# A second column piece of 36 instead of 26 in the score matmuls of 90-row blocks

## The chip, the cores and the metric

The kernel runs on one core of a Trainium2 chip. The metric is the device time of one execution in microseconds (us). The kernel before takes 801.79 us, the median of three runs (801.49 to 802.13).

## The reference

Talking-heads attention is followed by a gated feed-forward layer. Batch is 4, heads 12, sequence 448, head dimension 64; the inputs are 32-bit floats.

```python
scores = scale * np.matmul(q, k.transpose(0, 1, 3, 2))
scores = np.einsum('bhij,hg->bgij', scores, w_pre)
attn = np.exp(scores - np.max(scores, axis=-1, keepdims=True))
attn = attn / (np.sum(attn, axis=-1, keepdims=True) + 1e-09)
attn = np.einsum('bhij,hg->bgij', attn, w_post)
x = np.matmul(attn, v)                      # then as 1792 x 768
gate = 1.0 / (1.0 + np.exp(-(x @ w_gate)))
out = gate * (x @ w_val) @ w_out
```

## The kernel before, in words

The attention comes first (up to about 345 us), the feed-forward layer after it. The query rows of each batch are cut into four blocks of 120, 120, 120 and 88 rows. Rows are worked on in sets of ten (`R`), so the last block of a batch holds nine sets and carries 90 rows, two of them twice. There are 16 blocks, and four of them (one for each batch) have 90 rows.

`scores(bi, c, sc)` (line 151) computes q times k for one block and one pair of heads. The two heads of a pair lie in partitions 0 to 63 and 64 to 127 of the tiles `q` and `k` (`e` is 0 or 1). The block's rows are the columns of the stationary operand. They are cut into two pieces, 0 to 64 and 64 to `n`, and the results of both pieces go to one PSUM bank, to partitions 0 to 63 and from 64 on. So one call issues four matmuls, piece by piece and in each piece head by head: (first piece, e=0), (first, e=1), (second, e=0), (second, e=1). A matmul of 32-bit floats appears as two weight loads and two matmul records in the trace, so one call, a "score group" below, has eight of each. A block has six groups. For blocks of 120 rows the second piece has 56 columns, for blocks of 90 rows it has 26.

`keep` (line 159) copies the first `n` rows of each score bank to SBUF (`st`), on ScalarE for e=0 and on VectorE for e=1. `regroup` (line 195) lets DMAs on SyncE's queue bring `st` into the tile `T`, where heads and rows of two sets lie in the partitions; `premix` (line 205) mixes the heads by matmuls into the banks `pm`; `rowmax` takes the row maxima (VectorE, `nm`), `expo` the exponentials (ScalarE, `e`), `norm` and `scale` the division (GpSimd, `ss` and `ph`), `p_lo` the low part (VectorE, `pl`), `postmix` (line 243) mixes the heads again (TensorE, `mx`), `mix` (line 257) copies that out of PSUM (ScalarE), and `av` (line 272) multiplies by v, with its result copied out on ScalarE (`xt`).

All this runs in slots, one for each unit of two sets; the order inside a slot is written out by hand in the loop at line 396. In slot s TensorE gets premix(s+2), one score group of the next block but one, postmix(s), and one `av`, in this order. ScalarE gets the first exponential of s+2, the copy of scores, the second exponential, in some slots a sum of absolute values over v (`v_sum`, tile `v_abs`), then mix(s), and in some slots `xt`. `mx` is a single buffer, so postmix(s+1) starts when mix(s) is done. SyncE issues the loads of q, k, v and weights and the `regroup` DMAs in the order of the slots.

`q_load` (line 140) loads a block's q into a tile of 720 columns, of which a 90-row block uses 540 (pair c in columns 90c to 90c+89). There are two such tiles.

Of the kernel before, what the change touches and what calls it, by code (L numbers as in the profile page):

```python
# [32 lines left out]
def _sets(n):  # L33

    return [min(r0, n - R) for r0 in range(0, n, R)]
# [6 lines left out]
def _attention(ctx, tc, ins, B, H, S, D, xs, raws, make_moe):  # L42

    nc = tc.nc
    qp, kp, vb = (ins[n] for n in ("qp", "kp", "vb"))
    NQ = H // QUAD
    NP = H // 2
# [69 lines left out]
    for b in range(B):  # L117
        for i0, n in _blocks(S):
            rows = _sets(n)
# [13 lines left out]
    k_t, q_t = {}, {}  # L133
# [6 lines left out]
    def q_load(bi, eng=None):  # L140

        b, i0, _, _, sets = blocks[bi]
        n = R * sets
        t = qst.tile([128, NP * QB], F32, tag="q", name="q")
        (eng or nc.sync).dma_start(out=t[:, :NP * n], in_=qp[b, :, NP * i0:NP * (i0 + n)])
        q_t[bi] = t[:, :NP * n].rearrange("p (c s) -> p c s", s=n)


    st_t = {}
# [1 line left out]
    def scores(bi, c, sc):  # L151
        b, n = blocks[bi][0], R * blocks[bi][4]
        q, k = q_t[bi], k_t[b, c]
        for s0, s1 in ((0, 64), (64, n)):
            for e in range(2):
                rows = slice(64 * e, 64 * e + 64)
                nc.tensor.matmul(sc[e][s0:s1, :S], lhsT=q[rows, c, s0:s1], rhs=k[rows, :], start=True, stop=True)  # L157

    def keep(bi, c, e, sc):
        n = R * blocks[bi][4]  # L160
# [148 lines left out]
    for b in range(B):  # L309
# [3 lines left out]
        s = f + 5  # L313
        for i in range(H // 2):
            s = max(s + 1, f + 6 + 2 * (2 * i // QUAD))
# [10 lines left out]
    for bi in range(1, NBK):  # L326
        s0, s1 = first[bi - 1] - LEAD, first[bi] - LEAD
        for c in range(NP):
            at(spread(c, NP, s0, s1), scores, bi, c)
        if bi > 1:  # L330
            at(s0 - 4, q_load, bi)
    for bi in range(NBK):
        s0 = first[bi + 1]
        s1 = first[bi + 2] if bi + 2 < len(first) else s0
# [29 lines left out]

    k_load(0, 0, nc.sync)
    q_load(0, nc.sync)
    for c in range(1, NP):
        k_load(0, c, nc.sync)
    mix_in = load_mix()
    q_load(1, nc.scalar)  # L370
    warm(10)
    todo = []

    def ahead(c):
        if c % 3 == 0:
            mx = two_banks(ps_mx, "mx")
            sc = [mx[:, e] for e in range(2)]
        else:
            sc = pm[:2] if c % 3 == 1 else qk_banks()
        scores(0, c, sc)  # L380
        todo.append(sc)
# [14 lines left out]
    for s in range(min(min(plan), -LEAD), max(plan) + 1):  # L396
# [14 lines left out]
        def job(bi, c):  # L411
            sc = qk_banks()
            scores(bi, c, sc)
            return lambda e: keep(bi, c, e, sc)
# [56 lines left out]
class _Moe:  # L471
# [14 lines left out]
    NP = 7  # L486
# [797 lines left out]
```

## Time and profile before

| | |
|---|---|
| median of 3 runs | 801.79 us |
| the profiled execution | 802.14 us |
| its span from the first to the last instruction | 800.4 us |
| TensorE busy | 778.9 us |
| VectorE busy | 638.3 us |
| ScalarE busy | 566.1 us |
| GpSimd busy | 292.6 us |
| granted TensorE clock, mean | 0.996 |

The profile names engines PE (TensorE matmuls), PEld (its weight loads), DVE (VectorE), ACT (ScalarE), POOL (GpSimd) and SP (SyncE, which issues DMAs). A name such as L157 is a line of the kernel. A busy TensorE isn't one at its peak: matmuls overlap one another in the array, and a stretch in which they follow one by one counts as busy all the same. So of a group of matmuls the distance from its first start to the next group's start is to be read, and not the duration of one record.

### The profile page before, as it was taken

What the parts mean: (1) busy time and instruction counts of PE and PEld (TensorE: products, weight loads), DVE (VectorE), ACT (ScalarE), POOL (GpSimd) and SP (SyncE); (2) the same over time, 40 slices, a digit from 0 to 9 for tenths busy, and PEclk for the clock granted to TensorE, in tenths of its full rate; (3) what the DMA queues carried; (4) which work ended last, traced back from release to release, by engine and by line L of the source; (5) the groups of instructions that cost most, each with busy time, mean ns of one, the idle gap of its engine ahead of it and who ended that gap; (6) DMA issues with size and microseconds to landing.
All of it is one profiled execution on the core that took longest, in us unless ns stands there. A gap on an engine that the chain in (4) does not pass through costs nothing.

```text
span 800.4 us, 23490 instructions
## 1 busy us (share of the span) xinstructions
PE 778.9 (97%) x9626; PEld 418.8 (52%) x9626; DVE 638.3 (80%) x1068; ACT 566.1 (71%) x1106; POOL 292.6 (37%) x462
## 2 busy tenths in 40 slices
PE   8899999999999999978999999999999999999998
PEld 2445655555555655555555555555555555555554
DVE  4977999799978897889998989679886899997111
ACT  3887888888989898878876868568766784553000
POOL 1546666666765654420222232233322212010000
PEclk9999999999999999989999999999999999999999
DMA  5786577757886474665725364665557788995001
GB/s 196 218 233 226 172 237 235 250 173 225 247 254 214 165 238 163 206 170 183 237 76 194 131 218 171 250 214 187 203 153 279 271 306 310 366 381 213 35 35 69
DMA packets 80715, 166.15 MB, mean 208 GB/s; under 512 B 20448, under 2 KB 57664, under 8 KB 80608
## 3 DMA queue, kind: packets, MB, share of 16 engines
q1 hardware_dynamic: 72304, 132.88, 50.6%
q0 software_dynamic: 7728, 31.27, 10.2%
q8 instruction: 75, 1.23, 0.6%
q10 hardware_dynamic: 576, 0.51, 0.2%
q14 instruction: 32, 0.26, 0.1%
HBM read 87.77 MB, written 38.15 MB: 157 GB/s over the span
## 4 chain that ended last, share of the span: by engine, by line
PE 84%; ACT 7%; DVE 5%; DMA 1%; issue 1%; POOL 1%; SPq 0%; ACTq 0%; DVEq 0%; POOLq 0%
PE bank L1138 34%; PE bank L1149 18%; PE qk L157 9%; PE av L280 9%; PE pm L211 7%; PE mx L253 6%; ACT e L223 3%; DVE nm L216 2%; ACT mix L261 1%; DVE pl L241 1%; ACT st L163 1%; ACT m L1117 1%; DVE m L1122 1%; DMA k<-in_kp_dram 1%; DVE st L163 0%
## 5 line engine op out<-in xcount | busy, mean ns | idle before, releaser
L1138 PEld LDWEIGHTS <-m 128*128 128x128 f16 x1512 | 147.8, 98 | 142.1 <-DVE m L1122 3.5
L1138 PE MATMUL bank<-m,m 128*128 128x448 f16 x1116 | 214.4, 352 | 2.7 <-DVE m L1122 2.6
L223 ACT ACTIVATE e<-pm,nm 128x448 f32<-128x448 f32 x180 | 115.2, 641 | 46.8 <-DVE nm L216 44.0
L235 POOL TENSOR_SCALAR ph<-e,ss 128x448 f16<-128x448 f32 x180 | 113.3, 641 | 50.3 <-DVE ss L229 32.8
L216 DVE TENSOR_REDUCE nm<-pm 128x1 f32<-128x448 f32 x180 | 103.5, 616 | 23.9 <-PE pm L211 22.6
L241 DVE SCALAR_TENSOR_TENSOR pl<-e,ss,ph 128x448 f16<-128x448 f32 x180 | 120.8, 710 | 1.2 <-POOL ph L235 1.2
L157 PE MATMUL qk<-k,q 64*64 64x448 f32 (+1 forms) x736 | 112.6, 541 | 2.1 <-ACT st L163 2.1
L1149 PEld LDWEIGHTS <-m 128*128 128x128 f16 x756 | 74.0, 98 | 69.0
L253 PEld LDWEIGHTS <-ph 64*128 64x128 f16 x2880 | 64.6, 93 | 73.6 <-POOL ph L235 33.3
L261 ACT ACTIVATE mix<-mx 128x960 f32<-128x960 f32 (+1 forms) x92 | 102.9, 1119 | 0.2 <-PE mx L253 0.2
L211 PE MATMUL pm<-T,w 64*64 64x448 f32 (+1 forms) x720 | 95.2, 560 | 0.7 <-ACT e L223 0.7
L280 PE MATMUL av<-mix,v 128*64 128x120 f32 (+1 forms) x1504 | 93.3, 269 | 1.4 <-ACT xt L290 1.4
L1149 PE MATMUL bank<-m,m 128*128 128x448 f16 x468 | 92.9, 352 | 0.0
L1075 POOL CAST raws<-raws 128x768 f16<-128x768 bf16 x36 | 37.6, 1045 | 119.3 <-ACT raws L1069 119.3
L253 PE MATMUL mx<-w2hi,ph 64*128 64x60 f16 x1440 | 70.9, 188 | 8.8 <-ACT mix L261 8.5
L1138 PE MATMUL bank<-m 128*128 128x448 f16 x396 | 78.7, 355 | 0.0
L280 PEld LDWEIGHTS av<-mix,v 128*64 128x64 f32 x1504 | 74.1, 138 | 6.1 <-ACT xt L290 1.7
L228 POOL TENSOR_SCALAR ss<-ss 128x2 f32<-128x2 f32 (+1 forms) x92 | 37.4, 407 | 101.2 <-ACT e L223 99.6
L253 PE MATMUL mx<-w2hi,pl 64*128 64x60 f16 x1440 | 70.1, 187 | 0.8 <-DVE st L163 0.8
L253 PE MATMUL mx<-w2lo,ph 64*128 64x60 f16 x1440 | 70.2, 187 | 0.0
L163 DVE COPY st<-qk 120x448 f32<-120x448 f32 (+1 forms) x92 | 56.8, 618 | 13.5 <-PE qk L157 13.1
L1165 DVE TENSOR_TENSOR m<-bank,m 128x448 f32<-128x448 f32 x72 | 44.6, 621 | 22.9 <-PE bank L1138 14.7
(125 smaller groups left out, 1085.0 us busy)
## 6 DMA issues: line engine op xcount, KB each, us to landing
T<-st SPq DMA_DIRECT2D x176, 210.0 KB
m<-w SPq DMA_DIRECT2D x60, 384.0 KB
raws<-in_w_dram SPq DMA_DIRECT2D x28, 767.6 KB
hs<-m POOLq DMA_DIRECT2D x48, 224.0 KB, 3.5
m<-hs SPq DMA_DIRECT2D x15, 672.0 KB
w<-m POOLq DMA_DIRECT2D x21, 384.0 KB, 4.3
w<-raws POOLq DMA_DIRECT2D x20, 384.0 KB, 4.6
v<-in_vb_dram SPq DMA_DIRECT2D x12, 512.0 KB
```

Of the source, the lines that this page charges most:

```text
L157: nc.tensor.matmul(sc[e][s0:s1, :S], lhsT=q[rows, c, s0:s1], rhs=k[rows, :], start=True, stop=True)
L163: (nc.vector.tensor_copy if e else nc.scalar.copy)(st_t[bi][:n, 2 * c + e], sc[e][:n, :S])
L211: nc.tensor.matmul(pm[bank][64 * x:64 * x + 64, :S], lhsT=w1[rows], rhs=T[rows, x], start=True, stop=True)
L216: nc.vector.tensor_reduce(nm[:, i:i + 1], pm[bank][:, :S], axis=AX.X, op=ALU.max, negate=True)
L223: nc.scalar.activation(out=e_t[u][:, i], in_=pm[units[u][2][i]][:, :S], func=AF.Exp, bias=nm_t[u][:, i:i + 1], scale=1.0, accum_out=ss_t[u ...
L235: nc.gpsimd.tensor_scalar(ph[:, i], e_t[u][:, i], ss_t[u][:, i:i + 1], 1.0, op0=ALU.mult, op1=ALU.mult)
L241: nc.vector.scalar_tensor_tensor(pl[:, i], e_t[u][:, i], ss_t[u][:, i:i + 1], p_t[u][0][:, i], op0=ALU.mult, op1=ALU.subtract)
L253: nc.tensor.matmul(mx[:, x, i, jb * HK:(jb + 1) * HK], lhsT=p[rows, i, JB[jb]:JB[jb] + 128], rhs=w[rows], start=(k == 0), stop=(k == 2))
L261: nc.scalar.activation(out=out.rearrange("p g (y r) -> p y g r", r=HALF), in_=mx_t.pop(u), func=AF.Copy, scale=1.0 / (P_UP * W_UP))
L280: nc.tensor.matmul(av_t[bi][64 * i:64 * i + 64, c % 4, :n], lhsT=vt[b, u][:, h + i, jb, :], rhs=mixes[bi % 2][:, jb, 2 * c + i, :n], start ...
L1138: self.nc.tensor.matmul(self.f32(bank), lhsT=w[a][:, k], rhs=x[b][:, k], start=self.START[i] and k == r == 0, stop=k == self.KH - 1 and r ...
L1149: self.nc.tensor.matmul(self.f32(bank), lhsT=w[a][:, k], rhs=b[bb], start=self.START[i] and j == k == r == 0, stop=j == OUT_TILES - 1 and ...
```

## The change

For blocks of fewer than 100 rows the second column piece of the scores ends at column 100 instead of 90: it is 36 columns wide instead of 26. The ten further columns belong to the next pair of heads in the q tile; for the last pair they lie behind the loaded data, and a new GpSimd memset sets these ten columns to zero. The further results go to partitions 90 to 99 of the score banks, and `keep` doesn't copy them. Blocks of 120 rows issue what they did before.

```diff
@@ q_load
-        q_t[bi] = t[:, :NP * n].rearrange("p (c s) -> p c s", s=n)
+        if n < 100:
+            nc.gpsimd.memset(t[:, NP * n:NP * n + 100 - n], 0.0)
+        q_t[bi] = [t[:, c * n:] for c in range(NP)]
@@ scores
-        for s0, s1 in ((0, 64), (64, n)):
+        for s0, s1 in ((0, 64), (64, max(n, 100))):
             for e in range(2):
                 rows = slice(64 * e, 64 * e + 64)
-                nc.tensor.matmul(sc[e][s0:s1, :S], lhsT=q[rows, c, s0:s1], rhs=k[rows, :], start=True, stop=True)
+                nc.tensor.matmul(sc[e][s0:s1, :S], lhsT=q[c][rows, s0:s1], rhs=k[rows, :], start=True, stop=True)
```

## Rows read from the trace of the kernel before

**Rows 1.** The page: busy time by engine, and the chain of waits by engine.
```profile
PE 778.9 (97%) x9626; PEld 418.8 (52%) x9626; DVE 638.3 (80%) x1068; ACT 566.1 (71%) x1106; POOL 292.6 (37%) x462
PE 84%; ACT 7%; DVE 5%; DMA 1%; issue 1%; POOL 1%; SPq 0%; ACTq 0%; DVEq 0%; POOLq 0%
```

**Rows 2.** Groups by shape, line 157: count | busy us, mean ns | idle before.
```profile
L157 PE MATMUL qk<-k,q 64*56 64x448 f32 x272 | 65.3, 540 | 0.0
...
L157 PE MATMUL qk<-k,q 64*26 64x448 f32 x96 | 22.5, 545 | 0.0
...
L157 PEld LDWEIGHTS qk<-k,q 64*56 64x56 f32 x272 | 17.8, 127 | 0.0
...
L157 PEld LDWEIGHTS qk<-k,q 64*26 64x26 f32 x96 | 3.1, 99 | 16.9 <-issue 16.9
```

**Rows 3.** Timeline of PE, two slots with 120-row scores: start us, us, what.
```profile
252.56 0.93 PE L157 MATMUL qk<-k,q 64*64 64x448 f32 x8
253.42 0.20 PE L253 MATMUL mx<-w2hi,ph 64*128 64x60 f16 x2
...
255.96 0.93 PE L157 MATMUL qk<-k,q 64*64 64x448 f32 x8
```

**Rows 4.** Timeline of PE, then PEld, a slot with 90-row scores.
```profile
139.20 1.79 PE L157 MATMUL qk<-k,q 64*64 64x448 f32 x8
...
143.46 0.92 PE L157 MATMUL qk<-k,q 64*64 64x448 f32 x4
...
140.05 0.13 PEld L157 LDWEIGHTS qk<-k,q 64*26 64x26 f32 x4 [0.70 <-issue]
```

**Rows 5.** Four 90-row windows, one 120-row: busy PE, PEld, DVE, ACT, POOL; clock, DMA.
```profile
44.87:71.35 26.48, 25.72 (x485) 12.97 (x483) 18.81 (x37) 22.34 (x50) 14.03 (x21) 1.00 0.77 221
130.69:156.23 25.54, 25.54 (x485) 12.92 (x483) 19.78 (x40) 22.30 (x53) 15.45 (x24) 1.00 0.83 259
215.31:240.87 25.56, 25.56 (x484) 12.96 (x482) 19.67 (x40) 21.47 (x53) 15.75 (x24) 1.00 0.83 250
299.43:324.98 25.55, 25.55 (x484) 12.77 (x478) 19.68 (x45) 22.26 (x49) 11.54 (x18) 1.00 0.45 156
246.00:263.00 17.00, 17.00 (x412) 10.70 (x408) 15.18 (x31) 15.49 (x36) 10.69 (x19) 1.00 0.62 197
```

**Rows 6.** Timeline of ACT, one 90-row slot and the next one's start.
```profile
146.94 1.11 ACT L261 ACTIVATE mix<-mx 128x960 f32<-128x960 f32 x1
148.72 0.63 ACT L223 ACTIVATE e<-pm,nm 128x448 f32<-128x448 f32 x1 [0.66 <-DVE nm L216]
...
149.53 0.53 ACT L163 COPY st<-qk 90x448 f32<-90x448 f32 x1
...
151.19 1.12 ACT L261 ACTIVATE mix<-mx 128x960 f32<-128x960 f32 x1
152.17 0.44 ACT L290 ACTIVATE xt<-av,sw 128x240 f32<-128x240 f32 x1
```

**Rows 7.** Waits in 215.31:240.87: us in total, times, longest us.
```profile
PEld pm L211 <- DMA T<-st: 0.6, 1, 0.6
```

**Rows 8.** Groups: the memsets on POOL.
```profile
L193 POOL MEMSET T<- 4x896 f32 x4 | 3.2, 835 | 0.3 <-POOLq L1270 0.3
...
L1270 POOL MEMSET const-float32-1.0<- 128x1 f32 x1 | 0.1, 99 | 0.0
```

**Rows 9.** Timeline, POOL and SP around the third 90-row load of q.
```profile
202.29 0.62 SPq L145 DMA_DIRECT2D q<-in_qp_dram  x1
202.60 1.26 POOL L235 TENSOR_SCALAR ph<-e,ss 128x448 f16<-128x448 f32 x2 [0.37 <-DVE ss L229]
```

**Rows 10.** The page, DMA issues: KB each, median us to landing.
```profile
w<-raws POOLq DMA_DIRECT2D x20, 384.0 KB, 4.6
```

**Rows 11.** Windows: early slots with an idling PE, and the attention's end.
```profile
25.49:41.00 15.51, 13.80 (x327) 8.04 (x325) 15.08 (x32) 14.31 (x31) 7.98 (x15) 1.00 0.73 210
350.00:360.00 10.00, 6.94 (x144) 5.70 (x136) 8.36 (x10) 8.69 (x13) 2.43 (x4) 0.72 0.18 54
```

## The prediction

> **What bounds the kernel now.** I read the page first, then the groups of line 157 with shapes kept apart, then the timeline of TensorE around one score group of each kind, then the busy time by stretch, and last what ScalarE and the DMA queues do in the stretches that change. The page says that TensorE is busy for 97% of the span and that 84% of the chain of waits lies on it [rows 1]. That alone doesn't say that its time is well spent. The groups by shape look harmless too: a score matmul with 26 columns takes 545 ns, one with 56 columns 540 [rows 2]. What differs is when they start. In a 120-row slot the whole score group lasts 0.93 us, and postmix starts 0.86 us after the group's start [rows 3]: all four matmuls of a pass run side by side. In a 90-row slot the group lasts 1.79 us [rows 4], and its narrow weight loads stand idle for 0.70 us until the first piece has run through. So the 26-wide piece doesn't run beside the 64-wide one; it runs after it. The 96 narrow weight loads together show 16.9 us of such idle time [rows 2].
>
> The same 0.86 us stands in the slot's period: 4.26 us from score group to score group with 90 rows (139.20 to 143.46), 3.40 us with 120 rows (252.56 to 255.96) [rows 3, 4]. TensorE shows no idle time in three of the four 90-row stretches, and 0.76 us in the first [rows 5]. These stretches are thus bound by TensorE today, and by a TensorE that does two things one after the other which it does at once elsewhere.
>
> **What the change removes.** 96 records of the 26-wide matmul, four for each group, make 24 groups. If the 36-wide piece runs beside the 64-wide one as the 56-wide does, each group loses 1.79 - 0.93 = 0.86 us, in all 24 x 0.86 = 20.6 us of TensorE time. The trace has no piece of 36 columns. The bounds are nothing (it behaves as 26) and 0.86 us (it behaves as 56). I take the latter, though 26 is the nearer number: what the two rows differ in is whether the piece runs beside a 64-wide one, and more columns can only take it toward the kind that does. The duration of a record doesn't grow (540 against 545 ns) and a weight load, between 99 ns (26 columns) and 127 (56) [rows 2], lies under running matmuls in the 120-row slots, so it costs nothing there. If that cover were missing, 96 loads by 0.03 us would be 3 us.
>
> The Trainium skill, TensorEngine Tiling (Array Packing), sections "Available Configurations" and "Key Properties", lists column tiles of 128, 64 and 32 and says that a change of the tiling mode, not merely of the tile, drains the engine. By it 26 columns make a 32-wide tile and 36 a 64-wide one, which is the mode of the first piece, and the sum would be the full 0.86 us a group. No run here shows a width between 26 and 56.
>
> **What is late next.** ScalarE. In a 90-row slot with `v_abs` it goes from mix to mix in 4.25 us (146.94 to 151.19) and waits 0.66 us of that for the row maxima [rows 6], which wait for TensorE. That leaves 3.59 us; about 0.1 of it is the copy `st` standing for the end of the score group, since it starts 0.81 us after an exponential that lasts 0.63. So ScalarE needs some 3.5 us where TensorE would need 3.40, and where an `xt` of 0.44 us follows mix [rows 6], up to 3.9. `mx` has one buffer, so a late mix holds the next postmix and with it all of TensorE. Over a whole stretch: ScalarE is busy for 22.34, 22.30, 21.47 and 22.26 us [rows 5], with seven mixes where six belong to six slots; less one of 1.12 us [rows 6] that is 20.3 to 21.2 us. TensorE would need 25.55 - 6 x 0.86 = 20.4 us. The two take turns in being late, and neither fills the other's gaps entirely, so I take 21.5 us, 0.3 above ScalarE's own work. A stretch then gains 25.55 - 21.5 = 4.05 us, the first one as much (its 0.76 us of waiting stays), and four gain 16.2 us. VectorE's 19.8 us [rows 5] fit in 21.5.
>
> The same page of the Trainium skill, section "PSUM Bottleneck", says that tiling speeds up TensorE but not the copies out of PSUM, which may become the bottleneck. The rows on ScalarE agree, and by them 4.4 of the 20.6 us are lost.
>
> **The DMA queues** come after that. They are busy for 0.77, 0.83, 0.83 and 0.45 of these stretches [rows 5]. The same packets in 21.5 us would take 0.83 x 25.55 / 21.5 = 0.99 in the second and the third. The third already has one wait of premix for its DMA, 0.6 us [rows 7], so there is no reserve there. The cost lies between nothing (loads slide into the emptier slots that follow, 0.62 in a 120-row stretch [rows 5]) and the whole gain of those two, 8.1 us. I take 1.8 us, an estimate: 1.2 in the third, twice its wait of today, and 0.6 in the second. That leaves 16.2 - 1.8 = 14.4 us.
>
> **What it adds.** Four memsets of 128 x 10 on GpSimd. The nearest rows are 99 ns for 128 x 1 and 835 ns for 4 x 896 [rows 8]; I take 0.1 us. GpSimd is busy for 63% of a 120-row stretch [rows 5], so this is hidden; without that cover it would be at most 4 x 0.84 = 3.3 us, and it can't gain, being work added. The memset also stands in GpSimd's queue behind `scale` and ahead of later `norm` and `scale`. Its tile was last read by scores some three slots earlier, so it waits for nothing there. If it waited for the q load before it, though, GpSimd would stand: in the third case SyncE issues that load at 202.29 and `ph` ends at 203.86 [rows 9]; with the 4.6 us that a DMA of 384 KB takes to land [rows 10] that is some 3 us, and `ph`, `pl` and postmix behind it. The columns are disjoint, so I take nothing and keep 4 x 3 = 12 us as the other end. The last pair's second piece waits for the memset, three slots and more after it; nothing. Copies still take 90 rows, so no engine but TensorE has more to write.
>
> **The sum.** The profiled run of before took 802.14 us, a span of 800.4 and 1.7 around it; 802.14 - 14.4 = 787.7. It lies 0.35 above the median, so against the median the forecast is 787.4 us. What follows the attention is moved, not changed: it is bound by TensorE or by its own waits.
>
> **The rivals.**
> 1. TensorE alone bounds: ScalarE's and the DMAs' excess is absorbed by neighbouring slots. 801.8 - 20.6 = 781.2 us. For it: TensorE, VectorE and ScalarE all run nearly full in 120-row slots already. Against it: the single buffer of `mx`.
> 2. DMAs bound the second and third stretch, which keep 1 us of gain each, and the first keeps 3: 801.8 - (3 + 1 + 1 + 4) = 792.8 us. For it: 0.99 of the queues and the wait [rows 5, 7]. The memset that waits for its load would end in the same place or a little lower.
> 3. 36 columns don't run beside 64 either: 801.8 us. For it only that no row shows this width.
> 4. Slower: TensorE, no longer bound, idles for ScalarE, and the chip grants it the half clock. It does so once, at the attention's end, where the mean is 0.72 with TensorE busy for 6.94 of 10 us [rows 11]. A slot of 3.40 us at 1.2 GHz takes 3.40 us more, so 14.4 / 3.4 = 4.2 of the 24 slots decide; half of them would end at 787.4 + 12 x 3.4 = 828 us. Against it: between 25 and 41 us TensorE was busy for 13.80 of 15.51 us, idler than it would be here, at a clock of 1.00 [rows 11].
>
> **How the numbers follow.** Forecast (ScalarE and some DMA) 0.64, its own range 784.5 to 790.5; rival 1 0.11; rival 2 0.14; rival 3 0.08; rival 4 0.03. The range from 781.5 to 793.5 takes in the forecast and most of rivals 1 and 2 and leaves out 3 and 4 and some of the tails, about 0.18. A measurement of this kernel can tell about 0.2% (1.6 us) from no change. Faster: 0.64 + 0.11 + 0.14 = 0.89; same 0.08; slower 0.03.
>
> **What would show it.** The score group of 90 rows lasts 0.93 us and the idle time of its narrow weight loads is gone: else the first step is wrong. Stretches of six slots take 21.5 us, with new waits of postmix for mix: 20.4 would mean rival 1. Waits of premix for T in the second and third stretch above 2 us in all mean rival 2. A wait of the memset for the q load, or a clock under 1.00 in these stretches, would be a cost that I put at nothing. The gain must stand whole at the attention's end; if the end of the program moves by less, the step "moved, not changed" fails.

## The result

The changed kernel takes 789.19 us, the median of five runs (787.11 to 791.72), where the kernel before took 801.49 (800.71 to 802.13) on the same chip: a ratio of 0.9847 with a 95% interval of 0.9825 to 0.9870, a gain of 12.3 us. The forecast was 787.4 us with a range of 781.5 to 793.5 and 0.89 for faster. The profiled execution of after is the slowest of the five (791.72 us, span 789.9), so a second sample of the same kernel stands among the experiments (e5_again).

The page of after, busy time by engine and the chain of waits, answers to [rows 1]:

```profile
PE 763.4 (97%) x9626; PEld 419.5 (53%) x9626; DVE 637.1 (81%) x1068; ACT 562.3 (71%) x1106; POOL 287.6 (36%) x466
...
PE 75%; ACT 10%; DVE 6%; DMA 5%; POOL 2%; issue 2%; SPq 0%; ACTq 0%; DVEq 0%; POOLq 0%
```

TensorE's busy time fell by 15.5 us, and its share of the chain from 84% to 75%. What rose are DMA (1 to 5%) and ScalarE (7 to 10%). The lines of the code stand two further down than before (L157 is L159, L163 is L165, L261 is L263).

The score matmuls by shape, against [rows 2] (count | busy us, mean ns | idle before):

```profile
L159 PE MATMUL qk<-k,q 64*56 64x448 f32 x272 | 65.3, 540 | 0.0
L159 PE MATMUL qk<-k,q 64*36 64x448 f32 x96 | 22.2, 538 | 0.0
...
L159 PEld LDWEIGHTS qk<-k,q 64*36 64x36 f32 x96 | 5.8, 113 | 1.5 <-issue 0.9
```

The record of the narrow piece lasts as long as it did (538 against 545 ns). What is gone is the idle time ahead of its weight loads, 1.5 us instead of 16.9. The timeline of TensorE in a slot with scores of 90 rows shows the same, against [rows 4] (start us, us, what):

```profile
135.62 0.93 PE L159 MATMUL qk<-k,q 64*64 64x448 f32 x8
136.48 0.20 PE L255 MATMUL mx<-w2hi,ph 64*128 64x60 f16 x2
...
139.02 0.78 PE L159 MATMUL qk<-k,q 64*64 64x448 f32 x4
```

The group lasts 0.93 us, postmix starts 0.86 us after it, and this slot's period is 3.40 us: all three are the numbers of a 120-row slot [rows 3].

The four stretches with scores of 90 rows, cut at the starts of the same score groups as in [rows 5] (window, length; busy PE, PEld, DVE, ACT, POOL; clock, DMA share, GB/s). Behind the last group of the fourth no score group follows; that stretch ends where one would start, 0.81 us after the start of the next premix, which gives the 324.98 of [rows 5] in the kernel before:

```profile
44.94:67.88 22.94, 21.59 (x483) 12.87 (x479) 18.43 (x36) 20.67 (x50) 11.55 (x20) 1.00 0.82 231
128.41:150.34 21.93, 21.15 (x483) 13.25 (x479) 19.39 (x39) 20.41 (x51) 13.89 (x23) 1.00 0.88 275
209.76:234.78 25.02, 22.70 (x485) 13.27 (x481) 19.70 (x40) 20.83 (x53) 16.37 (x24) 0.93 0.79 247
293.35:314.54 21.19, 20.66 (x484) 12.28 (x476) 18.80 (x43) 20.91 (x49) 9.44 (x18) 1.00 0.52 175
```

They were 26.48, 25.54, 25.56 and 25.55 us long. So they gained 3.54, 3.61, 0.54 and 4.36 us, 12.05 in all. Between them the other slots lost: from the end of the first to the start of the second it is now 60.53 us (67.88 to 128.41) where it was 59.34, then 59.42 where it was 59.08, then 58.57 where it was 58.56, together 1.54 us. The start lost 0.07, and what follows the last stretch 0.02. The sum is 10.42 us, the difference of the two spans (800.36 and 789.94). The second and the fourth stretch are near the 21.5 us of the forecast; the third kept nearly nothing of the gain. Three places tell why.

First, ScalarE, which keeps even the undisturbed fourth stretch above the 20.4 us that TensorE would need. A slot of the second stretch, from mix to mix (start us, us, what):

```profile
138.89 1.13 ACT L263 ACTIVATE mix<-mx 128x960 f32<-128x960 f32 x1
139.87 0.65 ACT L292 ACTIVATE xt<-av,sw 128x480 f32<-128x480 f32 x1
...
142.04 0.66 ACT L178 ACTIVATE v_abs<-v 128x512 bf16<-128x512 f32 x1
...
142.65 1.15 ACT L263 ACTIVATE mix<-mx 128x960 f32<-128x960 f32 x1
```

Nothing stands in brackets, also on the lines left out: ScalarE works without a pause for 3.76 us from one mix to the next, where it waited 0.66 us in a slot of before [rows 6]. It is the late engine of such a slot. TensorE's waits for mix between 44 and 322 us, before and after (us in total, times, longest), are the sign that the prediction named for this:

```profile
PE mx L253 <- ACT mix L261: 0.9, 4, 0.3
...
PE mx L255 <- ACT mix L263: 3.3, 13, 0.3
```

Second, the first stretch. ScalarE's timeline, TensorE's, and SyncE's issues:

```profile
65.59 0.46 ACT L292 ACTIVATE xt<-av,sw 128x240 f32<-128x240 f32 x1 [1.67 <-DMA xs<-xt]
```

```profile
66.10 1.04 PE L282 MATMUL av<-mix,v 128*64 128x120 f32 x16 [1.08 <-ACT xt L292]
```

```profile
59.25 0.39 SPq L271 DMA_DIRECT2D xs<-xt  x1
```

The buffer of `xt` is free once the store of its last content has landed. That store was issued at 59.25 and still held the buffer at 65.5; ScalarE stood for 1.67 us, and TensorE, which needs the bank that `xt` empties, for 1.08. The kernel before had a wait of this kind too, once between 44 and 322 us, and after has two (us in total, times, longest):

```profile
ACT xt L290 <- DMA xs<-xt: 0.7, 1, 0.7
...
ACT xt L292 <- DMA xs<-xt: 2.7, 2, 1.7
```

Third, the third stretch. TensorE's timeline:

```profile
222.41 0.43 PE L282 MATMUL av<-mix,v 128*64 128x120 f32 x4
224.79 1.47 PE L282 MATMUL av<-mix,v 128*64 128x120 f32 x12 [1.95 <-issue]
226.19 1.77 PE L213 MATMUL pm<-T,w 64*64 64x448 f32 x8
```

The window around the place (columns as for the stretches):

```profile
224.00:228.10 4.10, 3.31 (x24) 1.86 (x28) 0.20 (x2) 1.12 (x3) 3.13 (x5) 0.58 0.74 265
```

In the middle of an `av` TensorE stops for 1.95 us, and no engine and no data DMA is named for it ("issue": no releaser shows). At its end the granted clock falls to half: a mean of 0.58 over 4.10 us is some 3.4 us at 1.2 GHz, in which premix takes 1.77 us instead of 0.98. The wait and half of 3.4 us, an estimate of what the half clock cost, come to 3.65 us, all that this stretch has over 21.4.

### The profile page after: what moved, and what is told of

Same layout as the page of the kernel before. It is cut to its first block, busy times and chain, and to the rows that moved or that the text cites. A ratio compares the mean times of both kernels' runs of the same rounds, so it can differ in the third digit from the quotient of the medians.

```text
span 789.9 us, 23497 instructions
## 1 busy us (share of the span) xinstructions
PE 763.4 (97%) x9626; PEld 419.5 (53%) x9626; DVE 637.1 (81%) x1068; ACT 562.3 (71%) x1106; POOL 287.6 (36%) x466
## 3 DMA queue, kind: packets, MB, share of 16 engines
q8 instruction: 75, 1.23, 0.7%
## 4 chain that ended last, share of the span: by engine, by line
PE 75%; ACT 10%; DVE 6%; DMA 5%; POOL 2%; issue 2%; SPq 0%; ACTq 0%; DVEq 0%; POOLq 0%
PE bank L1140 34%; PE bank L1151 18%; PE av L282 7%; PE pm L213 6%; PE qk L159 5%; PE mx L255 5%; ACT e L225 4%; ACT mix L263 2%; DVE nm L218 2%; DMA T<-st 2%; DMA xs<-xt 2%; DVE pl L243 1%; ACT st L165 1%; ACT v_abs L178 1%; DVE m L1124 1%
## 5 line engine op out<-in xcount | busy, mean ns | idle before, releaser
L263 ACT ACTIVATE mix<-mx 128x960 f32<-128x960 f32 (+1 forms) x92 | 103.0, 1119 | 0.2 <-PE mx L255 0.2
L213 PE MATMUL pm<-T,w 64*64 64x448 f32 (+1 forms) x720 | 97.5, 565 | 0.7 <-ACT e L225 0.7
L159 PE MATMUL qk<-k,q 64*64 64x448 f32 x736 | 95.1, 540 | 2.0 <-ACT st L165 1.8
L230 POOL TENSOR_SCALAR ss<-ss 128x2 f32<-128x2 f32 (+1 forms) x92 | 30.8, 335 | 95.7 <-ACT e L225 94.0
L1167 DVE TENSOR_TENSOR m<-bank,m 128x448 f32<-128x448 f32 x72 | 44.6, 621 | 22.7 <-PE bank L1140 14.4
L255 PEld LDWEIGHTS <-pl 64*128 64x128 f16 x1440 | 61.4, 93 | 0.0
```

What stands on the lines that cost most here:

```text
L159: nc.tensor.matmul(sc[e][s0:s1, :S], lhsT=q[c][rows, s0:s1], rhs=k[rows, :], start=True, stop=True)
L213: nc.tensor.matmul(pm[bank][64 * x:64 * x + 64, :S], lhsT=w1[rows], rhs=T[rows, x], start=True, stop=True)
L255: nc.tensor.matmul(mx[:, x, i, jb * HK:(jb + 1) * HK], lhsT=p[rows, i, JB[jb]:JB[jb] + 128], rhs=w[rows], start=(k == 0), stop=(k == 2))
L263: nc.scalar.activation(out=out.rearrange("p g (y r) -> p y g r", r=HALF), in_=mx_t.pop(u), func=AF.Copy, scale=1.0 / (P_UP * W_UP))
L1167: self.nc.vector.tensor_tensor(self.f32(out), self.f32(bank), self.f32(snap), op=ALU.add)
```

## The experiments

Their stretches, in us, from the same windows as above, and the sum of the three pieces between them (each window is cut at the starts of the same score groups, the end of the fourth as said above):

| kernel | 1st | 2nd | 3rd | 4th | between | time, median |
|---|---|---|---|---|---|---|
| before | 26.48 | 25.54 | 25.56 | 25.55 | 176.98 | 801.49 |
| after | 22.94 | 21.93 | 25.02 | 21.19 | 178.52 | 789.19 |
| e5_again (after once more) | 21.89 | 22.73 | 22.90 | 21.20 | 179.01 | 789.36 |
| e2_w33 (33 wide) | 21.43 | 21.48 | 24.03 | 21.26 | 177.90 | 788.12 |
| e3_vlate (sums of v later) | 21.76 | 23.15 | 24.97 | 20.43 | 181.01 | 794.90 |
| e4_kearly (k loaded earlier) | 23.74 | 21.20 | 25.51 | 21.22 | 178.22 | 790.38 |
| e6_no_vsum | 22.12 | 20.70 | 23.10 | 21.37 | 177.14 | 787.25 |
| e7_no_reload | 22.91 | 21.38 | 22.03 | 21.20 | 178.94 | 788.10 |
| e8_no_both | 22.32 | 20.42 | 21.91 | 20.42 | 178.83 | 787.21 |
| e9_xfer_after | 21.20 | 25.92 | 24.07 | 21.65 | 178.39 | 791.10 |
| e10_xfer_before | 25.54 | 25.54 | 25.54 | 25.55 | 177.00 | 801.52 |
| e11_half_sums | 21.07 | 21.36 | 24.34 | 21.59 | 180.77 | 791.11 |

### Where does a piece begin to run beside its neighbour?

```diff
-        if n < 100:
-            nc.gpsimd.memset(t[:, NP * n:NP * n + 100 - n], 0.0)
+        if n < 96:
+            nc.gpsimd.memset(t[:, NP * n:NP * n + 96 - n], 0.0)
...
-        for s0, s1 in ((0, 64), (64, max(n, 100))):
+        for s0, s1 in ((0, 64), (64, max(n, 96))):
```

That is e1_w32, a second piece of 32 columns. e2_w33 has 97 in the place of 96, a piece of 33.

> The second piece is 32 columns wide. Theory one (a piece of up to 32 columns can't run beside a 64-wide one, whatever its exact width): the score group of 90 rows still lasts 1.79 us and the time is that of before, 801.5 us. Rival (more columns help by degrees, or any width above 26 will do): the group is shorter, some 0.9 to 1.4 us, and the time lies between 789 and 796 us.

> The second piece is 33 columns wide, one more than in the run before it. Theory one (32 is the edge): the score group lasts 0.93 us and the time is that of the changed kernel, 787 to 791 us. Rival (the edge lies elsewhere, between 33 and 36): 1.79 us and 801.5 us.

Measured: 801.16 us with 32 columns (ratio 0.9997, 0.9987 to 1.0006) and 788.12 with 33 (0.9845, 0.9820 to 0.9871). The score matmuls by shape, with 32 columns:

```profile
L159 PE MATMUL qk<-k,q 64*32 64x448 f32 x96 | 22.6, 548 | 0.0
L159 PEld LDWEIGHTS qk<-k,q 64*32 64x32 f32 x96 | 3.4, 104 | 16.9 <-issue 16.9
```

and with 33:

```profile
L159 PE MATMUL qk<-k,q 64*33 64x448 f32 x96 | 22.1, 536 | 0.0
L159 PEld LDWEIGHTS qk<-k,q 64*33 64x33 f32 x96 | 5.6, 108 | 1.0 <-issue 0.7
```

One column turns the 16.9 us of idle weight loads into 1.0, and 13.0 us of the kernel's time go with it. The edge lies between 32 and 33, and at this edge the time is a step: 32 columns cost what 26 did, 33 gain what 36 do. The Trainium skill, TensorEngine Tiling (Array Packing), section "Available Configurations", lists column tiles of 32, 64 and 128. The step agrees with it: up to 32 columns make one kind of tile, from 33 on the kind that the first piece has. What exactly makes the narrow piece wait isn't shown; the runs show that it waits, and at which width it stops.

### Is it the sums over v, or the loads of k?

e3_vlate moves the six sums of |v| of each batch behind the slots with 90-row scores:

```diff
-        s = f + 5
+        s = f + 12
...
-            s = max(s + 1, f + 6 + 2 * (2 * i // QUAD))
+            s = s + 1
```

e4_kearly moves the loads of k out of the slots ahead of and in the stretches:

```diff
-            at(spread(c, NP, first[PB * (b - 1)] + 6, first[PB * b - 1] - LEAD - 2), k_load, b, c)
+            at(spread(c, NP, max(first[PB * (b - 1)] - 10, 1), first[PB * (b - 1)] + 6), k_load, b, c)
```

> The changed kernel, with the six sums of absolute values over v of each batch moved behind the slots with 90-row scores, into 120-row slots. Theory one (ScalarE is what is late in the 90-row slots): slots that take 3.4 and 3.65 us in turn go to 3.40, each of the four stretches gains 0.5 to 1 us, and the time falls by 2 to 4 us against the changed kernel. Theory two (the DMA queues are what is late): under 1 us.

> The changed kernel, with the k loads of the second to fourth batch issued some 11 to 16 slots earlier, out of the 90-row slots. Theory one (ScalarE alone costs the missing part): under 1 us. Theory two (full DMA queues in the first three 90-row stretches hold premix, the copy out of av and the instructions of TensorE): the waits for T and for xs vanish, the third stretch loses its stall, and the time falls by 3 to 5 us against the changed kernel, to 784 to 786.

Measured: 794.90 us for the later sums (ratio 0.9930, 0.9907 to 0.9954), worse than the changed kernel; 790.38 for the earlier loads (0.9868, 0.9839 to 0.9898), no difference that can be told. The window of e3_vlate's fourth stretch:

```profile
296.27:316.70 20.43, 20.43 (x484) 11.99 (x476) 18.75 (x42) 17.55 (x39) 9.53 (x18) 1.00 0.56 187
```

The window of e4_kearly's third stretch, and from its timeline TensorE's longest wait there:

```profile
209.97:235.48 25.51, 22.78 (x485) 13.27 (x481) 19.79 (x40) 21.12 (x53) 15.56 (x24) 0.93 0.66 207
```

```profile
225.47 0.83 PE L282 MATMUL av<-mix,v 128*64 128x120 f32 x10 [2.16 <-issue]
```

Neither theory had forecast a loss for the later sums. With ScalarE rid of the sums (17.55 us busy instead of 20.91), the fourth stretch goes at TensorE's pace. But the sums are only elsewhere: the slots between the stretches grow by 2.5 us against the changed kernel (181.01 against 178.52), so in these slots ScalarE had no room for them either. That is less than the 5.7 us between the medians; what makes up the rest isn't shown. In e4_kearly the third stretch keeps its long wait "issue", in the same `av` as in the changed kernel and two weight loads later, with the DMA share down from 0.79 to 0.66; and the first stretch grows to 23.74 us, with waits of premix for T of 0.67 and 0.42 us. So the average load of the queues in a stretch doesn't decide on that wait.

### The changed kernel again, without the sums, without the reloads, without both

e5_again is the changed kernel. e6_no_vsum leaves out the sums:

```diff
+    nc.gpsimd.memset(vm, 64.0)
...
-            at(s, v_sum, b, i)
```

e7_no_reload leaves out 20 loads of raw weights (the diff without the lines that keep the conversions of these tiles off the part of the buffer that is read):

```diff
     def early(self, k, step):
         raw = self.free["R"][k % len(self.free["R"])]
+        if step < 4 and k >= 3:
+            return
         if step < 4:
...
```

e8_no_both is both edits together.

> The changed kernel itself once more, so that the next three kernels stand beside it and the place of its losses is seen twice. If the losses belong to the program (the instructions and their order), the stretches are 21.4 to 22.9, 21.5 to 21.9, 24 to 25 and 21.5 to 21.7 us again, with the long wait of TensorE near the middle of the third. If they belong to chance, the long wait is somewhere else or gone, and the third stretch is near 21.5 to 22.

> The changed kernel without the 24 ScalarE sums over |v| (v_sum is left out, and its bound comes from a constant, so the scale of part of the later work is another). A sum costs ScalarE 0.65 + 0.20 = 0.85 us. Theory ACT (ScalarE sets the 90-row slots once the groups are short): every undisturbed 90-row slot falls from the mix of 3.42 and 3.57 to 3.78 us to the 3.40 us that TensorE alone wants, the fourth stretch from 21.65 to 20.4 to 20.8 us; the whole gains 2 to 5 us on the changed kernel, 783 to 787. Rival PE (the groups set the slots, the gaps are something else): slots and time as in the changed kernel. Rival DMA (transfers set them): the fourth stretch, where the transfers are light, gains, the first three do not, and the whole gains under 1.5 us.

> The changed kernel without the raw weight loads of the early tiles 3 to 7 (5 of 8 tiles, 20 DMAs of 192 KB, 3.8 MB): the tiles are converted from what tiles 0 to 2 left, with the same instructions on GpSimd, VectorE and ScalarE (the maxima of these tiles are those of tiles 0 to 2, and their copies hold old numbers). Theory DMA (what the first three stretches lose comes from transfers that land late, T, xs and TensorE's own instructions): the second and third stretch fall to 21.4 to 21.9 us, the wait of TensorE in the third shrinks under 0.7 us, the clock stays at 1.00 through attention, and the whole is 783 to 786.5 us. Rival program (the long wait stands at a place of the program whatever the transfers do): the third stretch stays at 24 to 25 us and the time at 787 to 790.

> Both left out at once: the sums over |v| and the raw weight loads of the early tiles 3 to 7. If ScalarE and the transfers are the two things that keep the kernel from what TensorE alone would give (24 groups x 0.86 = 20.6 us under the kernel before, 781.2 us on its profiled execution), this kernel gives 779 to 783 us, with the last three stretches at 20.4 to 21.0 us. If a third thing holds it, it stays above 784 us.

Measured, all beside the same runs of before: 789.36 us (ratio 0.9854, 0.9837 to 0.9871), 787.25 (0.9826, 0.9803 to 0.9849), 788.10 (0.9844, 0.9818 to 0.9870) and 787.21 (0.9832, 0.9810 to 0.9854). On the whole time no one of the edits can be told from the changed kernel with certainty; the intervals overlap. The stretches say more. TensorE's timeline in the third stretch of e5_again:

```profile
224.12 0.73 PE L282 MATMUL av<-mix,v 128*64 128x120 f32 x10 [0.96 <-issue]
```

The four windows of e8_no_both:

```profile
45.22:67.54 22.32, 20.81 (x482) 12.93 (x478) 18.42 (x36) 17.12 (x39) 11.96 (x20) 1.00 0.84 235
127.36:147.78 20.42, 20.42 (x484) 12.14 (x480) 19.07 (x40) 18.29 (x43) 13.64 (x23) 1.00 0.85 273
206.81:228.72 21.91, 21.25 (x484) 12.86 (x480) 17.92 (x38) 17.60 (x41) 16.98 (x23) 1.00 0.80 259
288.70:309.12 20.42, 20.42 (x484) 11.99 (x476) 18.86 (x43) 17.50 (x39) 9.37 (x18) 1.00 0.51 177
```

Without sums and reloads the second and the fourth stretch both take 20.42 us, with TensorE busy from end to end: the 20.4 us that TensorE alone was worked out to need. With the sums and without the reloads (e7_no_reload) they take 21.38 and 21.20, so the sums on ScalarE cost 0.8 to 1.0 us of a stretch. Leaving out the sums alone shows it less well: e6_no_vsum gets 20.70 in the second, but 21.37 in the fourth, more than with the sums, where 20.4 to 20.8 was expected; its first two slots there are long (4.0 and 3.8 us), the other three 3.40, and I have found no cause for that.

The third stretch is 21.91 and 22.03 us in the two kernels without the reloads, and 22.90 to 25.51 in the eight with the short groups and the reloads (25.02, 22.90, 24.03, 24.97, 25.51, 23.10, 24.07, 24.34). Premix's waits for T, in TensorE's weight loads between 44 and 322 us, are 0.8 us in all without the reloads and 0.5 without both; in the eight they are 1.6 to 6.5. That is the theory DMA. Its other half failed, though: e7_no_reload was to be at 783 to 786.5 us and isn't. It lost in its first stretch what it gained in the third, by a wait "issue" of 1.48 us at 52.37, like that of the changed kernel at another place, and e8_no_both lost in its first by the wait that the changed kernel has there too (timelines of ScalarE and TensorE):

```profile
65.25 0.46 ACT L293 ACTIVATE xt<-av,sw 128x240 f32<-128x240 f32 x1 [2.59 <-DMA xs<-xt]
```

```profile
65.77 1.04 PE L283 MATMUL av<-mix,v 128*64 128x120 f32 x16 [1.51 <-ACT xt L293]
```

Nor is e8_no_both at 779 to 783 us: it stays above 784, so by what was said ahead of it a third thing holds it. Its first stretch has 1.9 us more than TensorE needs, its third 1.5, and the slots between the stretches 1.9 more than before.

And e5_again answers what it was asked: the wait in the third stretch stands at the same instruction in both samples, 1.95 and 0.96 us long; at 0.96 us the clock stayed at full speed. In these two the place is the program's and the length varies. In the kernel with 33 columns, whose program differs by three columns alone, no wait "issue" above 0.2 us stands in the third stretch, and it takes 24.03 us all the same. TensorE's longest wait there is for T:

```profile
218.23 0.97 PE L213 MATMUL pm<-T,w 64*64 64x448 f32 x4 [0.88 <-DMA T<-st]
```

### More transfers, in the changed kernel and in the one before

```diff
+    def more_store(b, c):
+        nc.sync.dma_start(out=more[b, c], in_=vt[b, NQ - 1].rearrange("p h j d -> p (h j d)")[:, :420])
...
             at(spread(c, NP, s0, s1), scores, bi, c)
+            if R * blocks[bi][4] < 100:
+                at(spread(c, NP, s0, s1), more_store, blocks[bi][0], c)
```

e9_xfer_after has this on the changed kernel, e10_xfer_before on the one before.

> The changed kernel with one more transfer in each of the 24 slots with scores of 90 rows: 215 KB of a v tile are stored to a place in DRAM that nobody reads (SyncE's queue, as the T loads). At the rate of the changed kernel's second such stretch (275 GB/s at a busy share of 0.88, so some 310 GB/s at 1.0) six of them want 4.1 us of all 16 DMA engines in each stretch: 22.9, 23.4, 23.9 and 15.4 us of transfers against stretches that ScalarE would let pass in 21.5. Theory DMA (the first three stretches hang on the transfers once the groups are short, the fourth does not): the first three take 23 to 26 us, the fourth stays at 21.5 to 22.2, and the whole loses 3 to 8 us on the changed kernel, 792 to 797 us. Rival (the transfers have nothing to do with what the change lost): no stretch grows by over 0.5 us and the whole stays within 1 us, 788 to 790.

> The kernel before with the same 24 transfers more, the control for the other. Its stretches are 25.5 to 26.5 us long and the transfers in them would come to 23.8, 25.3, 25.3 and 15.6 us (busy shares 0.77, 0.83, 0.83 and 0.45 of rows 5, and 4.1 us more). Theory DMA: there is room for nearly all, the stretches grow by 0 to 1.5 us in the second and third, and the whole loses 0 to 3 us, 801 to 804 us, less than the changed kernel loses. Rival: both kernels lose the same.

Measured: 791.10 us (ratio 0.9879, 0.9860 to 0.9898), 1.7 above e5_again, and 801.52 us (1.0006, 0.9991 to 1.0021), 0.2 above before. The 1.7 us are within what the runs leave open: the intervals of the changed kernel (0.9825 to 0.9870, and 0.9837 to 0.9871 in e5_again) overlap with this one. The windows of the changed kernel with the transfers:

```profile
45.69:66.89 21.20, 20.63 (x482) 12.43 (x478) 18.08 (x36) 20.54 (x50) 11.52 (x20) 1.00 0.88 281
126.87:152.79 25.92, 22.38 (x485) 13.46 (x480) 19.20 (x40) 21.84 (x53) 14.57 (x25) 0.94 0.89 288
212.27:236.34 24.07, 22.56 (x484) 12.88 (x480) 19.54 (x39) 20.65 (x51) 14.97 (x24) 1.00 0.91 289
295.27:316.92 21.65, 21.23 (x485) 12.44 (x482) 18.89 (x42) 20.87 (x49) 9.52 (x18) 1.00 0.67 218
```

and of the kernel before with them:

```profile
45.09:70.63 25.54, 25.54 (x484) 12.91 (x482) 18.81 (x37) 22.26 (x50) 14.03 (x21) 1.00 0.82 258
130.00:155.54 25.54, 25.54 (x484) 12.92 (x482) 19.77 (x40) 22.31 (x53) 15.46 (x24) 1.00 0.91 293
214.61:240.15 25.54, 25.54 (x485) 12.91 (x483) 19.77 (x40) 22.33 (x53) 16.69 (x25) 1.00 0.90 293
298.71:324.26 25.55, 25.55 (x484) 12.77 (x478) 19.69 (x45) 22.26 (x49) 11.54 (x18) 1.00 0.58 196
```

The kernel before takes 24 transfers more at a share of up to 0.91, and its second to fourth stretch don't move by more than 0.02 us (the first is without the wait of 0.76 us that it had [rows 5]). In the changed kernel, at 0.89, the second stretch grows to 25.92 us, and the store of `xt` does it again (timelines of ScalarE and TensorE in e9_xfer_after):

```profile
149.08 0.46 ACT L296 ACTIVATE xt<-av,sw 128x240 f32<-128x240 f32 x1 [3.57 <-DMA xs<-xt]
```

```profile
149.59 1.72 PE L286 MATMUL av<-mix,v 128*64 128x120 f32 x16 [2.77 <-ACT xt L296]
```

The first stretch, at 0.88, took no harm at all (21.20 us), and the third (24.07 us) lies between the two samples without the transfers (25.02 and 22.90). I had expected all three to grow by 1.5 us or more and the whole by 3 to 8. One of three grew, and on the whole time the sign isn't certain. So a loaded queue isn't a bound on the stretch's length by itself; that it makes a long landing likelier is what one stretch suggests, and isn't shown.

### Half of the sums on VectorE

```diff
+        o = vm[:, H // 2 * b + i:H // 2 * b + i + 1]
+        if i % 2:
+            nc.vector.tensor_reduce(o, v, axis=AX.X, op=ALU.add, apply_absolute_value=True)
+        else:
-        nc.scalar.activation(out=v_abs, in_=v, func=AF.Abs, accum_out=vm[:, H // 2 * b + i:H // 2 * b + i + 1])
+            nc.scalar.activation(out=v_abs, in_=v, func=AF.Abs, accum_out=o)
```

> The changed kernel with every second sum over |v| made by VectorE (a reduction of the absolute values, 128x512) instead of ScalarE: a candidate for a better kernel. ScalarE loses three of its six sums per stretch (3 x 0.85 = 2.6 us of some 20.4 to 21.3 busy), VectorE gains three reductions (the 128x448 row maximum takes 0.61 us, so about 0.7 us each by size, 2.1 us on some 19.4 to 19.7 busy). Theory ACT: the fourth stretch falls to 20.5 to 21.3 us and the whole to 785.5 to 788, half or more of what leaving out all sums gave. Rival DVE (VectorE becomes the late engine in its place): the stretches stay at 21.5 us or grow, 788 to 791.

Measured: 791.11 us (ratio 0.9875, 0.9861 to 0.9890). No gain; if anything 1.8 us are lost against e5_again. The fourth stretch is 21.59 us where it was 21.19 with all sums on ScalarE, with VectorE at 20.31 us instead of 18.80, and the slots between the stretches grew to 180.77 us, by 2.2 on the changed kernel. That agrees with the rival, by which VectorE has no more room than ScalarE; which wait holds TensorE there isn't shown. None of the kernels beats the changed one by more than the runs can tell.

## Why the prediction was right, and what was mis-sized

1. **The score group.** Right: 24 groups, 0.93 us each, and the idle time gone. The bound chosen (36 behaves as 56) was right; rival 3 is ruled out, and the edge at 32/33 shows by what: not by how near a width is to one row or the other.
2. **ScalarE is next late.** Right, in place and size. The fourth stretch, where the queues have room, is 21.19, 21.20, 21.26, 21.22, 21.20 and 21.65 us in the six kernels that leave ScalarE its sums in place (after, again, 33 wide, k earlier, no reloads, more transfers); 21.5 was forecast, mostly 0.3 too much. With the sums and reloads out it is 20.42, TensorE's own pace, so rival 1 would have needed a lighter ScalarE. The estimate of ScalarE's work (20.3 to 21.2 us) holds as well: 20.41 to 20.91.
3. **The DMA term** is the one that was mis-sized: 1.8 us, of which 1.2, "twice its wait of today", in the third stretch. The forecast without this term was 22.43 us for the first stretch (26.48 less 4.05) and 21.5 for each of the others, 86.9 in all. In the profiled execution of after they make 91.08, so 4.2 us were lost in them, and 1.5 between them, where nothing was forecast. In e5_again they make 88.72, and it is 1.8 and 2.0. Two reserves that weren't meant as such hid some of the cost, which is luck: undisturbed stretches take 21.2 to 21.4 us instead of 21.5, and the 0.76 us of waiting that the first was to keep didn't come again (21.20 us in e9_xfer_after). I looked for the loss at premix's waits for T [rows 7], and these stayed small in the profiled execution: 1.7 us in seven waits of weight loads over all of 44 to 322 us, where before had 1.0 in four. In the two samples of the changed kernel the larger part came at two places to which I had given no price: the single buffer of `xt`, whose store lands late (a wait of 0.7 us in the trace of before was the sign of it), and TensorE's own instructions. In six other kernels with short groups and the reloads, though, the waits for T did grow, to 3.0 us and more in all (3.2 with 33 columns, 6.5 with the later sums): the place that I named counts as well, and which of the three is hit varies from run to run. That the reloads are the common root is borne out for the third stretch only (without them 21.9 and 22.0 us). The share forecast for the third, 0.99, wasn't reached (0.79): when a wait lengthens the stretch, the share falls, so a share worked out from equal packets in less time tells that a wait will come, not how long it is.
4. **Rival 2** gave 792.8 us, the profiled execution took 791.7, but it had two stretches at 24.5 us and one that kept 3 of its 4 us. What came was one stretch that kept nearly nothing, in this execution, and smaller losses in two of them in the other (22.73 and 22.90 us).
5. **The half clock** (rival 4, 0.03) came once inside the stretches, for some 3.4 us, right behind the wait of 1.95 us, and again in e4_kearly behind one of 2.16 us (clock 0.93 in that window) and in e9_xfer_after behind one of 2.77 (0.94). It didn't spread: the short pauses for mix, 0.3 us each, left the clock at 1.00 in all other stretches. It was an unpriced part of the DMA term, 1.7 us by the estimate above, not a mechanism that turns the sign.
6. **The memset.** Right: 0.4 us in all, 108 ns each against 0.1 taken, and no wait ahead of it:

```profile
L147 POOL MEMSET q<- 128x10 f32 x4 | 0.4, 108 | 0.0
```

7. **"Moved, not changed."** Right within 0.02 us: 10.44 us had been saved at the end of the fourth stretch (324.98 to 314.54), and 10.42 at the program's end. In e5_again what follows was 0.8 us shorter than before.

So the forecast's 14.4 us became 12.3. The sum was right up to ScalarE (16.2 us). What comes behind it cost 3.9 us by the medians, and 5.7 in the profiled execution of after, rather than 1.8. The forecast came near because this one term was small beside the rest.

## What to carry to other kernels

Where two column pieces share the array, look at the distance between group starts and at the idle time of the narrow piece's weight loads, not at the durations of records: 32 columns beside 64 ran one after the other, 33 ran side by side, for the price of a few columns that nobody reads. Before you count the gain, go through the engines in the order of their slack, and then through every single buffer that a DMA must empty: a kernel whose slack is gone can feel landings that were hidden before. A control with the same added load on the old kernel is what can separate "the queues are full" from "nothing covers them any more": here the old kernel's stretches didn't move at a share of 0.91, and in the new one a single stretch did.

## What the runs showed of the hardware that I had not expected

**TensorE probably runs out of instructions.** The page of after has queues for them; this is the largest, and below it the same queue in a window of 1.4 us (221.9 to 223.3) at the start of the long wait (packets, MB, share of 16 engines):

```profile
q8 instruction: 75, 1.23, 0.7%
```

```profile
q8 instruction: 1, 0.02, 5.8%
```

1.23 MB in 75 packets are 16 KB each. TensorE has 9626 weight loads and 9626 matmuls, so one packet stands for some 257 of them. The packet in the window from 221.9 to 223.3 us is the only one between 215.8 and 228.5; TensorE stands from 222.84 to 224.79. In e5_again one lies between 221.40 and 222.65 and TensorE goes on at 224.12, at the same instruction; in e4_kearly, where it stops two weight loads later, between 222.85 and 224.05, and TensorE goes on at 225.47. The windows are cut closely around the packet, and each time the engine resumes 1.4 to 1.5 us after the window's end: the later the packet, the later TensorE. Nor is it this place alone. All traces of the case together have ten waits "issue" of TensorE above 0.4 us between 44 and 322 us, at several places and in six of the runs with short groups, and each of the ten ends 1.39 to 1.55 us after the end of such a packet; the kernel before, the one with 32 columns and the one before with more transfers have none. That the wait is one for instructions is inferred from these times; it wasn't tried by itself, since no run changed the instruction stream's length or place. The Trainium skill, Runtime: NRT & Kernel Launch, section "Instruction fetch mechanics", says that instructions are fetched in blocks of 16 KiB (256 instructions) by a DMA queue of the sequencer's own, and that the cost of a block's boundary is mostly hidden. The size agrees, and so does "mostly hidden": the kernel before has the same 75 packets and no such wait above 0.4 us. If they are waits for instructions, a boundary cost up to 2.16 us here while SyncE's queue was loaded.

**A store of `xt` held its buffer for some 6 us in such a stretch:** it was issued at 59.25 and the buffer was free at about 65.5. ScalarE's wait for it was 1.67 us in this run, 2.59 in e8_no_both and 3.57 in e9_xfer_after, at the same kind of place.

**The time may have become less steady.** Five runs of the changed kernel spread over 4.6 us (787.11 to 791.72), those of before beside them over 1.4 (800.71 to 802.13). But the four of e5_again spread over 2.1, and thirteen of before, beside the kernel with 32 columns, over 2.8; with more transfers the ten of before spread over 4.7 (799.39 to 804.04), although their median didn't move. A possible reason, which no run tests, is that slack beside a slow TensorE hides late landings until the queues are fuller.
